# A written list of 1,373 steps in place of the list scheduler, and the first chunk loaded in three pieces

## The chip, the core and the metric

The kernel runs on one core of one Trainium2 chip. Its engines are TensorE (PE, which multiplies matrices into the eight PSUM banks), VectorE (DVE), ScalarE (ACT), GpSimd (POOL) and SyncE (SP, which here only issues transfers). Each engine works through its own list of instructions in order, and the engines wait for each other through semaphores. The metric is the device time of one execution in microseconds (us).

## The reference

```python
for t in range(S):                                   # gated linear attention
    state = alpha[:, :, t, :, None] * state + np.einsum('bhd,bhe->bhde', k[:, :, t], v[:, :, t])
    y[:, :, t] = np.einsum('bhd,bhde->bhe', q[:, :, t], state)
...
x = y.transpose(0, 2, 1, 3).reshape(B, S, H * D)     # then a mixture of 4 attention experts
logits = x @ w_gate                                  # the best 2 of 4, softmax over the two
for e in range(E):
    q = x @ wq[e]; k = x @ wk[e]; v = x @ wv[e]
    a = softmax(causal(scale * (q @ k.transpose(0, 2, 1))))
    out += weight[e] * (a @ v @ wo[e])
```

B is 4, H 8, S 768, D 48; the second part is 384 wide with 4 experts of 64.

## The kernel before

The sequence of every batch is cut into 6 chunks of 128 positions, 24 chunks in all, numbered n. Three chunks make a unit u of 384 positions, so there are 8 units and two to a batch. The work is about 1,370 small steps, each of one engine. In the text a step is called by the key that it has in the code:

- For chunk n, `La`, `Lq` and `Lv` load the gates, q with k, and v. DVE then prepares q and k: `r` and `c` are scans of the gates (L163, with a reciprocal L169 between them), `k` (L182) and `q` (L187) multiply by their results. `e` is a small copy on POOL. For n >= 3 `cp` moves a part of the tile T by two small transfers. Chunk 0 is prepared in pieces, so its steps carry a piece number.
- `a` (L204) forms the products of q and k on PE, the two `m` mask them (on DVE L208, or on ACT L212 and then POOL L216), `t` (L221) transposes k, `kt` (L225, L227) evicts it, `u` (L241) forms the chunk's addition to the state, `sa` (L254, DVE) and `S` (L258, POOL; L250 on DVE for the first) update the state, `y` (L280) is the chunk's output, `xh` (ACT) and `xl` (DVE L294) split it in a high and a low part. `ck` (ACT L196) is a check on the gates whose result is only needed at the end.
- `wqh`, `wql`, `wvh`, `wvl`, `woh`, `wol` split the weights in the same manner, once, near the start: the `h` on ACT (L672, L673, L678, L681), the `l` on DVE or POOL (L666, L674).
- For unit u, `p` (L303) is one of four q or k projections and `v` (L325) one of three v projections; `s` (L376) are scores, `rd`, `ex`, `n` and `ns` the softmax (DVE L388, ACT L399, DVE L405, POOL L411), `t` with four numbers (L426) transposes the probabilities, `to` evicts them into one of the buffers `at`, `o` (L451) multiplies them by v, `w` (L470) is the output projection, `wo` evicts and `st` stores it. `t4001` stands for unit 4, pair 0, tile 0, expert 1 of the pair.

What sets the order is the function `run`. It is a list scheduler that runs when the program is built: each step has a target time (made from the constants PACE and OFF), an estimated duration and the steps and buffers that it needs, and at each turn the step with the best mark is given to its engine, which sets the order of every queue, the engine of steps that have a choice, and the buffer of each tile. Where it reckons that PE would stand idle for longer than IDLE, it puts filler matmuls in (`warm`, L803, a 128x256 product whose result nobody reads). The loads of the start, 30 fillers and the order of the first transfers are written out in `opening`.

Of the kernel before, what the change touches and what calls it, by code (L numbers as in the profile page):

```python
# [33 lines left out]
PACE = 12.4037  # L34
PULL = {"P": 0.007, "V": 0.02, "A": 0.02, "G": 0.1134, "S": 0.1114}
SWITCH = 0.6006
CHANGE = {("t", "f"): 0.065, ("f", "t"): 0.0}
CHANGE.update({(x, "a"): 0.19 for x in "tfy"})
CHANGE.update({(x, "s"): 0.15 for x in "tfy"})
CHANGE.update({(x, "y"): 0.12 for x in "tfas"})  # L40
CHANGE.update({(x, "t"): 0.15 for x in "asy"})
CHANGE.update({(x, "f"): 0.2 for x in "asy"})
IDLE = 0.3647
SHARE = 0
HEAD = 0.0628
MARGIN = 0.3762
SLOW = 1.0555
OFF = dict(load=1.5592, prep=0.7084, a=-0.2534, y=0.0569, p=-0.066, pw=0.4525, v=-0.5128, g=0.5234, s=-0.069, step=0.9176, n=0.3117, tr=1.0059, o=0.2201, w=0.7913, wt=-1.9145, hp=1.0622, ck=0.6172, end=1.3946, hd=0.1337, sx=-0.1614, wo=0.0629, xo=-0.1397)
# [7 lines left out]
def tile_gla_moe(ctx: ExitStack, tc: tile.TileContext, qk_d, al_d, v_d, wqk_d, wv_d, wo_d, nat_d, vn_d, out_d):  # L56
# [32 lines left out]
    early = [[view(raw[0][:, 4 * CW * i:4 * CW * i + 4 * CW], 2, 2, CW) for i in (0, 1)]]  # L89
# [7 lines left out]
    def pieces(n):  # L97
        return [(0, 2), (2, 4)] if n == 0 else [(0, tiles(n))]
# [383 lines left out]
    def op(key, target, deps, alts, uses=(), take=(), mode="", land=0.0, lock=False):  # L482
        o = dict(key=key, target=target, deps=list(deps), alts=alts, uses=list(uses), take=list(take), mode=mode, land=land, lock=lock)
        ops.append(o)
        for n in o["uses"]:
            users[n] = users.get(n, 0) + 1
        return o
# [10 lines left out]
    def load_ops(n):  # L498
        z = (n - 3 - OFF["load"]) * PACE
        if n > HALF:  # L500
            op(("La", n, 0), z, [], [("S", 0.57, lambda: load_al(n, 0, SY))], [("al", n)], [("al", n)], land=3.7)
            op(("Lq", n, 0), z, [], [("S", 0.57, lambda: load_q(n, 0, SY))], [("T", n)], [("T", n)], land=4.2)
        if n >= HALF:
            op(("Lv", n), z, [], [("S", 0.57, lambda: load_v(n))], [("v", n)], [("v", n)], land=3.0)

    def scale(f, w, n, i):
        return [("V", dv(w), lambda: f(V, n, i))] + [("G", 0.12 + 0.0021 * w, lambda: f(G, n, i))] * (n < SHARE)

    def prep_ops(n):
        z = (n - 2 - OFF["prep"] + OFF["hp"] * max(0.0, 1.0 - (n - HALF) / 3) * (n >= HALF)) * PACE  # L510
        for i, (p0, p1) in enumerate(pieces(n)):
            k = p1 - p0
            past = [("c", n - 2, 0)] if n > 1 else []
            op(("r", n, i), z, [("La", n, i)] + past, [("V", 0.33 + 0.27 * k, lambda i=i: prep_r(n, i))], [("al", n)], lock=True)
            op(("e", n, i), z, [("r", n, i), ("Lq", n, i)], [("G", 0.19, lambda i=i: prep_e(n, i))], [("al", n), ("T", n)])
            op(("c", n, i), z, [("r", n, i)], [("V", 0.15 + 0.27 * k, lambda i=i: prep_c(n, i))], [("al", n)], lock=True)
            op(("k", n, i), z, [("r", n, i), ("Lq", n, i)], scale(prep_k, 128 * k, n, i), [("al", n), ("T", n)],
               lock=True)
            op(("q", n, i), z, [("c", n, i), ("Lq", n, i)], scale(prep_q, 128 * k, n, i), [("al", n), ("T", n)],
               lock=True)  # L520
        ready = [(x, n, i) for x in "ekq" for i in range(len(pieces(n)))]
        if n >= FIRST:
            op(("cp", n), z, ready, [("S", 1.15, lambda: spread(n))], [("T", n)], land=2.2)
            ready = [("cp", n)]
        op(("ck", n), z + OFF["ck"] * PACE, [(x, n, i) for x in "ekq" for i in range(len(pieces(n)))],
# [3 lines left out]
    def chunk_ops(n):  # L529
# [4 lines left out]
        head = OFF["hd"] if n < HALF else 0.0  # L534
        z = (n - 1 + OFF["a"] - head) * PACE
        op(("a", n), z, ready, [("P", 0.95, lambda: gla_a(n))], [("T", n)], [("pa", n, 0), ("pa", n, 1), ("ms", n)], "a")
        for s in (0, 1):
            op(("m", n, s), z, [("a", n)],
# [3 lines left out]
        if not last:  # L542
            op(("t", n), z, ready, [("P", 0.42, lambda: gla_t(n))], [("T", n)], [("pt", n)], "t")
            op(("kt", n), z, [("t", n)], either(gla_k, 448, n), [("pt", n)], [("kt", n)])
        z = (n + OFF["y"] - head) * PACE
        op(("y", n), z, [("m", n, 0), ("m", n, 1), ("Lv", n)] + ([("S", n)] if c else []),
           [("P", 1.55 if c else 0.95, lambda: gla_y(n))], [("T", n), ("v", n), ("ms", n)], [("py", n)], "y")
        zx = z + OFF["xo"] * PACE
        op(("xh", n), zx, [("y", n)], [("A", da(W3), lambda: gla_xh(n))], [("py", n), ("x", u)], [("x", u)] if g == 0 else [])
        op(("xl", n), zx, [("xh", n)], [("V", dv(W3), lambda: gla_xl(n))], [("py", n), ("x", u)])  # L550
        if not last:
            op(("u", n), z, [("kt", n), ("Lv", n)], [("P", 0.36, lambda: gla_u(n))], [("kt", n), ("v", n)], [("pu", n)], "y")
# [455 lines left out]
```

## Time and profile before

| | us |
|---|---|
| median of the runs shown (321.55 to 321.92) | 321.70 |
| the profiled execution | 322.28 |
| its span, first to last instruction | 320.5 |
| PE busy in the span | 307.3 |
| DVE busy | 266.7 |
| ACT busy | 195.3 |
| POOL busy | 125.2 |

The profiled execution is 0.58 us above the median of the runs, and 1.78 us of it lie outside the span. PE's ends are modelled, so a busy PE may still be one that waits a little.

### The profile page before, as it was taken

Reading aid. Unit: us, or ns where it says so; the run is one execution under the profiler, and the core shown is the slowest. Engines: PE = TensorE matmul, PEld = TensorE weight load, DVE = VectorE, ACT = ScalarE, POOL = GpSimd, SP = SyncE. Lnnn points to the kernel's source line nnn. Section 1 sums busy time; section 2 is a strip of 40 time slices with the busy share of each in tenths; the row PEclk is TensorE's granted clock in tenths of the full one; section 3 lists DMA queues with packets and bytes.
Section 4 is the critical chain, followed back from the end, with each engine's and each line's share of the span. In section 5 each row is a group of like instructions: output and inputs, shape, how many; then the busy total and the mean of one; then the engine's idle time right before and its main releaser. Section 6 shows DMA issues by size and latency. Waiting matters only on the chain.

```text
span 320.5 us, 11175 instructions
## 1 busy us (share of the span) xinstructions
PE 307.3 (96%) x4443; PEld 264.2 (82%) x4443; DVE 266.7 (83%) x767; ACT 195.3 (61%) x532; POOL 125.2 (39%) x205
## 2 busy tenths in 40 slices
PE   6798999999999999999999999999999999999992
PEld 4578988989897888889897887889897987878682
DVE  4997999999999999898998899898795785767840
ACT  1563657767674775557676685547584673457851
POOL 6351437514565372104363083405353070306420
PEclk9999999999999999999999999999999999999998
DMA  7994454724524514442534334322310000201001
GB/s 256 393 332 157 131 156 133 216 77 133 156 80 110 152 46 157 118 139 88 140 95 112 117 112 139 96 82 64 111 35 14 3 2 0 77 2 66 12 30 58
DMA packets 26638, 35.22 MB, mean 110 GB/s; under 512 B 2288, under 2 KB 22864, under 8 KB 26576
## 3 DMA queue, kind: packets, MB, share of 16 engines
q1 hardware_dynamic: 25744, 33.49, 34.1%
q10 hardware_dynamic: 832, 0.92, 0.9%
q8 instruction: 37, 0.61, 0.8%
q14 instruction: 25, 0.20, 0.2%
HBM read 27.61 MB, written 4.72 MB: 101 GB/s over the span
## 4 chain that ended last, share of the span: by engine, by line
PE 83%; DVE 11%; DMA 2%; issue 1%; ACT 1%; POOL 0%; ACTq 0%; SPq 0%; DVEq 0%; POOLq 0%
PE g L303 15%; PE g L426 12%; PE g L451 12%; PE g L376 9%; PE g L280 9%; PE g L325 8%; PE g L470 8%; PE g L204 5%; PE g L241 2%; PE g L221 2%; DMA at<-in_al_dram 2%; DVE a L388 2%; DVE a L163 2%; DVE T L187 1%; DVE T L182 1%
## 5 line engine op out<-in xcount | busy, mean ns | idle before, releaser
L411 POOL TENSOR_SCALAR a<-a,cf,gw 128x128 f32<-128x128 f32 (+5 forms) x96 | 72.6, 767 | 78.8 <-DVE cf L405 28.7
L399 ACT ACTIVATE a<-a,mx 128x256 f32<-128x256 f32 (+3 forms) x96 | 51.4, 536 | 6.9 <-DVE mx L388 6.7
L426 PE MATMUL g<-ident,a 128*128 128x128 f32 x336 | 52.7, 277 | 0.5 <-DVE at L227 0.4
L303 PE MATMUL g<-x,wqkh 128*128 128x384 f32 x192 | 51.9, 352 | 0.0
L426 PEld LDWEIGHTS g<-ident,a 128*128 128x128 f32 x336 | 39.2, 140 | 7.4 <-issue 4.9
L216 POOL TENSOR_SCALAR_AFFINE_SELECT ms<-ms 128x512 f32<-128x512 f32 x29 | 21.0, 733 | 56.0 <-ACT ms L212 56.0
L225 ACT ACTIVATE at<-g 128x512 f32<-128x512 f32 (+3 forms) x68 | 31.2, 473 | 17.1 <-PE g L426 15.7
L451 PE MATMUL g<-at,vg 128*32 128x384 f32 (+2 forms) x648 | 40.0, 389 | 0.0
L376 PE MATMUL g<-k,q 64*128 64x256 f32 (+3 forms) x384 | 39.2, 336 | 0.0
L227 DVE COPY at<-g 128x256 f32<-128x256 f32 (+3 forms) x60 | 27.6, 467 | 9.2 <-PE g L426 8.6
L451 PEld LDWEIGHTS g<-at,vg 128*32 128x32 f32 x648 | 19.3, 109 | 18.6 <-issue 14.8
L303 PEld LDWEIGHTS g<-x,wqkh 128*128 128x128 f32 x192 | 33.1, 189 | 1.2 <-DVE mx L388 0.4
L376 PEld LDWEIGHTS g<-k,q 64*128 64x128 f32 x384 | 28.6, 185 | 6.1 <-issue 2.2
L280 PE MATMUL g<-ms,v 128*32 128x128 f32 x768 | 33.0, 273 | 0.1
L303 PE MATMUL g<-x,wqkl 128*128 128x384 f32 x96 | 32.4, 338 | 0.0
L325 PE MATMUL g<-wvh,x 128*128 128x260 f32 x144 | 31.7, 295 | 0.3 <-DVE mx L388 0.3
L204 PE MATMUL g<-T 48*128 48x128 f32 x384 | 26.7, 277 | 4.2 <-DVE T L187 4.2
L204 PEld LDWEIGHTS g<-T 48*128 48x128 f32 x384 | 24.2, 187 | 6.2 <-DVE T L187 5.3
L388 DVE CUSTOM_DVE_ANT_0 a<-g,cmask 128x128 f32<-128x128 f32 (+3 forms) x64 | 28.2, 483 | 0.9 <-PE g L376 0.9
L470 PE MATMUL g<-woh,yy 128*128 128x384 f32 x96 | 27.9, 349 | 0.0
L258 POOL TENSOR_TENSOR S<-st,T 48x192 f32<-48x192 f32 x32 | 20.5, 639 | 16.0 <-DVE st L254 12.5
L212 ACT ACTIVATE ms<-g 128x512 f32<-128x512 f32 x29 | 16.4, 591 | 14.8 <-PE g L204 14.4
(113 smaller groups left out, 627.4 us busy)
## 6 DMA issues: line engine op xcount, KB each, us to landing
al<-in_al_dram SPq DMA_DIRECT2D x21, 387.0 KB, 3.8
T<-in_qk_dram SPq DMA_DIRECT2D x21, 384.0 KB, 4.1
v<-in_v_dram SPq DMA_DIRECT2D x24, 256.0 KB, 3.0
out_dram<-ot SPq DMA_DIRECT2D x22, 192.0 KB, 1.9
T<-T SPq DMA_DIRECT2D x42, 48.2 KB, 2.2
a<-in_al_dram SPq DMA_DIRECT2D x2, 516.0 KB, 6.8
T<-in_qk_dram SPq DMA_DIRECT2D x2, 512.0 KB, 7.5
at<-in_wqk_dram SPq DMA_DIRECT2D x1, 768.0 KB, 9.3
```

Of the source, the lines that this page charges most:

```text
L204: PE.matmul(pa[s][:, C * p:C * p + C], t[r:r + D, p, C:2 * C], t[r:r + D, p, 0:C], start=True, stop=True, tile_position=(r, 0))
L225: A.activation(out, src, AF.Copy)
L280: PE.matmul(o[32 * j:32 * j + 32, k], l, r, start=(i == 0), stop=(i == len(parts) - 1), tile_position=(0, 32 * j))
L303: PE.matmul(pj[:, :W3], w[:, kt, cs], x[:, kt, :], start=(i == 0), stop=(i == 8))
L325: PE.matmul(pv[:, 0:260], x[:, kt, 128 * i:128 * i + 128], w[:, kt, :], start=(m == 0), stop=(m == 8))
L376: PE.matmul(sc(u, pair, i, e, x, c1 - c0), q[r, i0, ts], k[r, i1, c0:c1], start=(y == 0), stop=(y == 2), tile_position=(64 * e, 0))
L388: V.tensor_tensor_reduce(a[:, c0:c1], src, cmask[:, 512 - c1 + c0:512], -1.0, mx[:, 0:1] if x else 3.0e38, OP.add, OP.min, mx[:, 1:2])
L399: A.activation(a[:, c0:c1], src, AF.Exp, bias=mx[:, 1:2], scale=-1.0 if last else 1.0, accum_out=sm[:, x:x + 1])
L411: G.tensor_scalar(a[:, 0:n], a[:, 0:n], CF[u % 2][:, 3 * pair + i, e:e + 1], gw[:, u, i, eg:eg + 1], op0=OP.mult, op1=OP.mult)
L426: PE.transpose(pt[:, 128 * (j - j0):128 * (j - j0) + 128], a[:, 128 * j:128 * j + 128], ident)
L451: PE.matmul(o[r:r + 32, lo:n1], v[:, j % 3, 64 * eg + x:64 * eg + x + 32], at(("at", u, pair, e))[:, min(j, 4), at_off(j) + lo:at_off(j) + ...
L470: PE.matmul(po[:, 0:DM], y[:, h, 128 * i:128 * i + 128], w[:, pair, :], start=(m == 0), stop=(m == 5))
```

## The change

The scheduler, its constants and all estimates of time are gone from the order. In their place stands the text QUEUES, a list of 1,406 words: the 1,373 steps, of which 28 come in two halves, and fillers at 5 places. Each word is an engine's letter and the number of a step (P PE, V DVE, A ACT, G POOL, S SP; `z11` is 11 fillers). The new `run` gives out the steps in just that order. A buffer is taken from the front of a list of free ones and goes to the back of it when its last user has been issued. Beside that:

- Chunk 0 is loaded and prepared in three pieces of one, two and one of its four tiles (OPEN) and not in two of two.
- The first transfers of SP come in another order (ORDER): the weights wv ahead of wqk.
- The check `ck` of the first three chunks has to come after `wqh` (LATE).
- The tile pools `at` and `q` have 3 and 2 buffers, and had 4 and 3.

```diff
-PACE = 12.4037
...
+OPEN = [(0, 1), (1, 3), (3, 4)]
+LATE = 'wqh'
+ORDER = [(0, 1), (1, 0), (0, 2), (1, 1), (2, 1), (2, 0), (1, 2), (0, 3), (2, 2)]
+UNITS = dict(a=7, at=3, ms=2, kt=2, x=2, q=2, k=4, yy=2, vg=3, T=4, al=3, v=3, ot=2, st=2)
+
+QUEUES = """
+S1 S4 V68 V70 V71 G69 V72 V73 V75 V78 G74 V76 V77 G79 V80 V81 V82 V94 P84 P87 G95 A85 V86 A88 V96 z1 P92 V97 G85 V98
...
-        return [(0, 2), (2, 4)] if n == 0 else [(0, tiles(n))]
+        return OPEN if n == 0 else [(0, tiles(n))]
...
-    def run(start, arrive):
...
+    def run():
         left = dict(users)
+        spare = {k: list(range(len(unit[k]))) for k in unit}
...
+        for word in QUEUES.split():
+            e, i = word[0], int(word[1:])
+            if e == "z":
+                warm(spare["g"][0], i)
+                continue
+            o = ops[i]
...
             for name in o["take"]:
                 pool = POOL.get(name[0], name[0])
+                where[name] = (pool, spare[pool].pop(0))
             alt[2]()
             for name in o["uses"]:
+                left[name] -= 1
+                if left[name] == 0:
+                    pool, i = where[name]
+                    spare[pool] += i if isinstance(i, tuple) else (i,)
```

On DVE, from the first instruction on, the preparation of chunk 0 stood so before (`at_63` holds the gates of chunk 0, `T_85` its q and k; the scans are called SCALAR_TENSOR_TENSOR here):

```order
L163 SCALAR_TENSOR_TENSOR at_63<-at_63,d1r 128x258
L169 RECIPROCAL d1c_109<-at_63 128x2
L163 SCALAR_TENSOR_TENSOR at_63<-at_63,d1c_109 128x258
L182 TENSOR_TENSOR T_85<-T_85,at_63 128x2x128
L163 SCALAR_TENSOR_TENSOR at_63<-at_63,d1r 128x258
L169 RECIPROCAL d1c_109<-at_63 128x2
L187 TENSOR_TENSOR T_85<-T_85,at_63 128x2x128
```

and stands so now (L215 are the scans, L234 and L239 the products):

```order
L215 SCALAR_TENSOR_TENSOR at_63<-at_63,d1r 128x129
L221 RECIPROCAL d1c_107<-at_63 128x1
L215 SCALAR_TENSOR_TENSOR at_63<-at_63,d1c_107 128x129
L234 TENSOR_TENSOR T_83<-T_83,at_63 128x128
L239 TENSOR_TENSOR T_83<-T_83,at_63 128x128
L215 SCALAR_TENSOR_TENSOR at_63<-at_63,d1r 128x258
L221 RECIPROCAL d1c_107<-at_63 128x2
```

The first piece is half as wide, and chunk 0 takes 15 instructions of DVE where it took 10.

On POOL, after the first small copies, the weights' low parts stood so before (`ms` are the masked products, `S` and `st` the state):

```order
L173 COPY T_86<-a 128x4
L216 AFFINE_SELECT ms_67<-ms_67 128x512 x2
L216 AFFINE_SELECT ms_68<-ms_68 128x512
L173 COPY T_87<-a 128x4
L216 AFFINE_SELECT ms_68<-ms_68 128x512
L258 TENSOR_TENSOR S_113<-st_97,T_87 48x4x48 x2
L666 TENSOR_TENSOR wvl<-at_65,wvh 128x780
L173 COPY T_88<-al_89 128x3
```

and stand so now (L225 is the copy, L268 the mask, L310 the state, L701 the weights):

```order
L225 COPY T_84<-a 128x4
L268 AFFINE_SELECT ms_66<-ms_66 128x512
L225 COPY T_85<-a 128x4
L268 AFFINE_SELECT ms_67<-ms_67 128x512 x2
L701 TENSOR_TENSOR wvl<-at_65,wvh 128x780
L310 TENSOR_TENSOR S_111<-st_95,T_85 48x4x48 x2
L701 TENSOR_TENSOR wqkl<-at_64,wqkh 128x3x256
L701 TENSOR_TENSOR wol<-at_65,woh 128x768
L225 COPY T_86<-al_87 128x3
```

One of the four masks has gone to DVE, wvl comes ahead of the state, and the splits wqkl and wol, which were DVE's, stand on POOL ahead of the copy for chunk 3.

On PE, in the middle of the program, unit 4's first transposes stood so before (`a` are probabilities, `T2` and `T3` the tiles of chunks 18 and 19, the first name the PSUM bank):

```order
L426 MATMUL g7_107<-ident_111,a_99 128x128 x2
L221 MATMUL g4_104<-ident_111,T2_87 128x112 x4
L426 MATMUL g0_100<-ident_111,a_99 128x128
L221 MATMUL g6_106<-ident_111,T3_88 128x112 x4
L426 MATMUL g7_107<-ident_111,a_99 128x128
L280 MATMUL g5_105<-ms1_68,v2_94 32x128 x4
```

and stand so now (L478 the transposes of probabilities, L273 that of k, L355 a projection):

```order
L478 MATMUL g6_104<-ident_109,a_97 128x128
L478 MATMUL g1_99<-ident_109,a_97 128x128
L273 MATMUL g0_98<-ident_109,T2_85 128x112 x4
L478 MATMUL g3_101<-ident_109,a_97 128x128 x2
L478 MATMUL g2_100<-ident_109,a_97 128x128 x2
L355 MATMUL g4_102<-x1_71,wqkh_128 128x384 x2
```

Before, the second transpose of unit 4's first pair (the last L426 row, t4001) writes the bank g7 of the transposes that ended unit 3 (the first row, t3121), with two `t` and t4000 between them. Now t4000 and t4001 stand together, the next tile's two follow after one `t`, and each of the six rows has a bank of its own.

## Rows read from the trace of the kernel before

**Rows 1.** The page: busy time and the chain by engine.

```profile
PE 307.3 (96%) x4443; PEld 264.2 (82%) x4443; DVE 266.7 (83%) x767; ACT 195.3 (61%) x532; POOL 125.2 (39%) x205
...
PE 83%; DVE 11%; DMA 2%; issue 1%; ACT 1%; POOL 0%; ACTq 0%; SPq 0%; DVEq 0%; POOLq 0%
```

**Rows 2.** Stretches of the span: length, then busy time (instructions) by engine.

```profile
0.00:27.10 27.10, 20.34 (x367) 16.45 (x368) 20.85 (x35) 12.61 (x22) 13.27 (x33) 1.00 0.89 313
27.10:51.00 23.90, 23.47 (x349) 21.27 (x348) 23.22 (x64) 14.03 (x39) 7.88 (x15) 1.00 0.54 157
51.00:304.00 253.00, 252.53 (x3567) 216.90 (x3563) 218.93 (x659) 162.28 (x457) 101.70 (x156) 1.00 0.30 88
304.00:315.00 11.00, 10.94 (x176) 9.54 (x168) 3.69 (x11) 5.93 (x15) 2.39 (x3) 1.00 0.08 25
```

**Rows 3.** All waits of PE: total, times, longest.

```profile
PE g L204 <- DVE T L187: 4.2, 4, 1.6
PE g L803 <- POOL ones L137: 1.5, 1, 1.5
PE g L241 <- issue: 1.0, 1, 1.0
PE g L426 <- DVE at L227: 0.4, 1, 0.4
PE g L325 <- DVE mx L388: 0.3, 1, 0.3
```

**Rows 4.** PE in order of time: start, duration, [idle before, releaser].

```profile
1.55 5.01 PE L803 MATMUL g<-d1r 128*128 128x256 bf16 x30 [1.55 <-POOL ones L137]
8.20 0.72 PE L204 MATMUL g<-T 48*128 48x128 f32 x8 [1.64 <-DVE T L187]
...
14.09 1.16 PE L204 MATMUL g<-T 48*128 48x128 f32 x16 [1.46 <-DVE T L187]
...
19.34 1.16 PE L204 MATMUL g<-T 48*128 48x128 f32 x16 [0.55 <-DVE T L187]
...
25.57 0.28 PE L241 MATMUL g<-v,kt 128*32 128x48 f32 x7 [1.03 <-issue]
25.78 1.59 PE L803 MATMUL g<-d1r 128*128 128x256 bf16 x13
27.13 0.37 PE L325 MATMUL g<-wvh,x 128*128 128x260 f32 x1
...
28.29 0.52 PE L303 MATMUL g<-x,wqkh 128*128 128x384 f32 x2
...
33.66 0.72 PE L803 MATMUL g<-d1r 128*128 128x256 bf16 x5
34.30 1.16 PE L204 MATMUL g<-T 48*128 48x128 f32 x16
```

**Rows 5.** DVE in order of time.

```profile
4.85 0.78 DVE L163 TENSOR_TENSOR_SCAN at<-at,d1r 128x258 f32<-128x258 f32 x1 [2.83 <-DMA at<-in_al_dram]
...
9.32 1.22 DVE L163 TENSOR_TENSOR_SCAN a<-a,d1r 128x516 f32<-128x516 f32 x1
...
11.94 1.06 DVE L182 TENSOR_TENSOR T<-T,a 128x512 f32<-128x512 f32 x1
...
16.19 1.47 DVE L163 TENSOR_TENSOR_SCAN a<-a,d1c 128x516 f32<-128x516 f32 x1
17.59 0.66 DVE L182 TENSOR_TENSOR T<-T,a 128x512 f32<-128x512 f32 x1
...
20.60 1.29 DVE L208 TENSOR_TENSOR ms<-g,mask 128x512 f32<-128x512 f32 x2
...
22.67 0.95 DVE L666 TENSOR_TENSOR wqkl<-at,wqkh 128x768 fp32r<-128x768 f32 x1
23.57 0.56 DVE L294 TENSOR_TENSOR x<-g,x 128x384 fp32r<-128x384 f32 x1
25.97 0.74 DVE L254 TENSOR_TENSOR st<-g,S 48x192 f32<-48x192 f32 x2 [1.84 <-PE g L241]
```

**Rows 6.** POOL in order of time.

```profile
11.19 2.30 POOL L216 TENSOR_SCALAR_AFFINE_SELECT ms<-ms 128x512 f32<-128x512 f32 x2 [0.40 <-ACT ms L212]
15.95 0.63 POOL L216 TENSOR_SCALAR_AFFINE_SELECT ms<-ms 128x512 f32<-128x512 f32 x1 [2.46 <-ACT ms L212]
...
20.28 1.09 POOL L258 TENSOR_TENSOR S<-st,T 48x192 f32<-48x192 f32 x2 [1.54 <-DVE st L254]
23.30 2.04 POOL L666 TENSOR_TENSOR wvl<-at,wvh 128x780 fp32r<-128x780 f32 x1 [1.92 <-issue]
```

**Rows 7.** PE in the middle: two of its longer waits, and t7100.

```profile
47.73 0.39 PE L325 MATMUL g<-wvh,x 128*128 128x260 f32 x1 [0.34 <-DVE mx L388]
...
190.87 0.30 PE L426 MATMUL g<-ident,a 128*128 128x128 f32 x1 [0.39 <-DVE at L227]
...
304.07 1.64 PE L426 MATMUL g<-ident,a 128*128 128x128 f32 x13
```

More of the change, by code (lines that the diff above doesn't have):

```diff
@@ L33 @@
 FIRST = 3
-PACE = 12.4037
[L35 to L48, printed above, removed]
@@ L480, in tile_gla_moe, with op @@
     ops, users = [], {}
-    def op(key, target, deps, alts, uses=(), take=(), mode="", land=0.0, lock=False):
-        o = dict(key=key, target=target, deps=list(deps), alts=alts, uses=list(uses), take=list(take), mode=mode, land=land, lock=lock)
+    def op(key, deps, alts, uses=(), take=(), mode="", land=0.0, lock=False):
+        o = dict(key=key, deps=list(deps), alts=alts, uses=list(uses), take=list(take), mode=mode, land=land, lock=lock)
         ops.append(o)
@@ L522, in prep_ops @@
         if n >= FIRST:
-            op(("cp", n), z, ready, [("S", 1.15, lambda: spread(n))], [("T", n)], land=2.2)
+            op(("cp", n), ready, [("S", 1.15, lambda: spread(n))], [("T", n)], land=2.2)
             ready = [("cp", n)]
-        op(("ck", n), z + OFF["ck"] * PACE, [(x, n, i) for x in "ekq" for i in range(len(pieces(n)))],
+        op(("ck", n), [(x, n, i) for x in "ekq" for i in range(len(pieces(n)))] + [(LATE,)] * (n < HALF),
            [("A", 0.28 + 0.0021 * 129 * tiles(n) * 0.8, lambda: check(n))], [("al", n)])
@@ L598, in back_ops @@
             first = hf or i == 0
-            z = (base + step * k) * PACE
             if hf:
@@ L615, in back_ops @@
                 time = sum(3 * max(c1 - c0, 256) / 2170 for ii in tiles3 for c0, c1 in widths(u, ii)) + 0.05
-                op(scored, z, need + past, [("P", time, lambda p=pair, l=tiles3: [score(u, p, ii) for ii in l])],
+                op(scored, need + past, [("P", time, lambda p=pair, l=tiles3: [score(u, p, ii) for ii in l])],
                    [("q", u, pair), ("k", b, pair)], take, "s")
@@ new lines, in run @@
+                spare[pool].remove(j)
+        begun = set()
+        for word in QUEUES.split():
[4 more added lines that the diff above has]
+            o = ops[i]
+            if i in begun:
+                next(alt[3] for alt in o["alts"] if len(alt) > 3)[2]()
+                continue
+            alt = next(alt for alt in o["alts"] if alt[0] == e)
+            if len(alt) > 3:
+                begun.add(i)
@@ L781, in run @@
-            if e == "G":
-                lock["G"].append((t, end))
-            if e == "P":
-                mode = o["mode"] or mode
-            end += o["land"]
-            for name in o["uses"]:
-                give(name, end, e)
-            if len(alt) > 3:
-                k = dict(key=o["key"], target=o["target"], deps=[("half", o["key"])], alts=[alt[3]], uses=[], take=[], mode="", land=0.0,
-                         lock=False, n=0)
-                done["half", o["key"]] = (end, e)
-                cand.append(k)
-                continue
@@ L794, in run @@
-            done[o["key"]] = (end, e)
-            todo -= 1
-            for w in waiting.get(o["key"], ()):
-                w["n"] -= 1
-                if not w["n"]:
-                    cand.append(w)
+            for name in o["uses"]:
+                left[name] -= 1
+                if left[name] == 0:
+                    pool, i = where[name]
+                    spare[pool] += i if isinstance(i, tuple) else (i,)
     def warm(i, k):
```

303 lines of the change are left out of this document (126 added, 177 removed).

## The prediction

> **What bounds the kernel now.** The page says that PE is busy for 307.3 of 320.5 us, and the chain that ended last runs 83% on PE and 11% on DVE [rows 1]. PE's work as such is the same after the change: the same products of the same shapes. So time can come only from where PE has nothing useful to do, and I read where that is. The table by stretches shows PE busy for 20.34 of the first 27.1 us, for 23.47 of the next 23.9, for 252.53 of 253 in the middle and for 10.94 of 11 at the end [rows 2]. The list of PE's waits says the same: 4.2 us before the products `a` of the first chunks, 1.5 before the first filler, 1.0 in an `u`, and 0.7 in all the rest [rows 3]. The first stretch also holds 68 of the fillers, so the opening is the place to look at first.
>
> The same table shows why the opening is slow. Through 27.1 to 51 us DVE is busy for 23.22 of 23.9 us [rows 2], and in PE's rows each of the first chunks' `a` (8.20, 14.09, 19.34) waits for DVE's product `q` [rows 4]. DVE starts when the first gates land, at 4.85, and has one pause in the opening, 1.84 us ahead of the row at 25.97 [rows 5]. Until some 50 us it is DVE's work that lets PE go on.
>
> A modelled end of a matmul hides short waits, so I also went through PE's rows start to start. Between v00 (27.13, [rows 4]) and the start of t7100 at 304.07 [rows 7] stand 292 steps. I compared each with the shortest time that the same step takes after the same kind of step. What they lie above that adds up to 4.1 us: 1.0 by 51 us, and 3.1 after it in some 25 pieces, of which the longest is 0.55 around the row at 190.87; the row at 47.73 shows the longest of the first kind [rows 7]. That is all that a better order can win in the middle.
>
> **The change, part by part.**
>
> Chunk 0 in three pieces. DVE takes 15 instructions for 10. A scan of 258 columns takes 0.78 and one of 516 takes 1.22 [rows 5], so a third piece costs what does not shrink with width, about 0.2 us for the first scan and 0.1 to 0.2 for each of the other four, 0.6 in all. Against it stands an earlier start: the first transfer is half as large. I take 0.25 us for that; the bounds are 0 and 0.45 (half of its 264 KB at the rate of the stretch, 313 GB/s [rows 2], is 0.42). So DVE is through with chunk 0 some 0.35 us later than now (9.32).
>
> From there I walked DVE's new queue with the durations of its old rows: `r` of chunk 1 to 11.0, the mask that has come from POOL (half of 1.29) to 11.7, `c` to 12.9, `k` and `q` to 14.2 (0.66 each) or 15.0 (1.06 each, as beside POOL's mask now [rows 5, 6]), chunk 2's scans with xl0 and the first state to about 19.5, `q` of chunk 2 to 20.1, sa1, wql and an eviction of 0.5 to 21.9, two masks to 23.1, xl1 to 23.6. The scans of chunk 3 follow at once; they start at 27.2 now. DVE has this room because wqkl and wol (0.95 each) have gone to POOL and because its pause of 1.84 us is filled.
>
> PE on this walk: y1 when the first state is there, at 19.5, to 21.0; t2 and a2 to 22.5; u2; then v00 at 22.9, and not at 27.13. Now v00 stands behind 13 fillers, which take from 25.78 to 27.13 although wvl, its last input, is ready at 25.34 [rows 4, 6]. That wait of 1.35 us goes for certain. `wvh` and wvl come earlier too: ACT does wvh right behind chunk 1's masks, since the checks `ck` have been put behind wqh, and wvl stands ahead of the state on POOL. PE then does y2 (needs the masks at 23.1 and the state S2, 1.09 behind sa1 [rows 6], at 21.7) and is through with it at about 25.5. Now it has done the same steps at 28.29, where p000 starts [rows 4]. The lead is 2.8 us. PE goes on with v01, p001, v02, p011, p000 and gets to a3 at about 33; chunk 3's spread lands at about 31.5, so nothing waits there. The fillers there are 4 for 5, worth 0.1. **The opening gives 2.8 us.** Below, the certain part is the 1.35 less 0.35 and some 0.3 lost elsewhere, 0.7; above, with the unhindered products and a start at 4.4, it is 4.0.
>
> POOL's added work: wvl takes 2.04 us, so wqkl and wol take about 2.0 each with their 768 columns [rows 6]. They stand between the state S2 (done at 21.7) and the copy `e` of chunk 3, so they end at 25.7. The copy has to be done before chunk 3's spread, which waits for DVE's `k` at about 28. That hides them with 2 us to spare. If that cover is gone, a3 is late by the excess, and the projections ahead of it hide another 1.5.
>
> The middle. Two things speak for less waiting. First, rows that wait now have another place: t4001 waits for DVE's eviction from the bank that t3121 has just left, 0.39 us [rows 7], and now writes a bank that none of the rows shown uses. Second, I counted PE's work between the score step and the transposes that need it, from the two orders with each step's present duration. Its median over 96 pairs is 9.5 us now and 13.7 us after, its smallest 4.1 and 5.5. More work stands between a step and the one that waits for its softmax. Against it: the buffers `at` are 3 for 4, so the pair's second transpose must follow the last pair's `o` on PE, and the order no longer adapts to anything. The shortest cover between a last transpose and its `o` is 0.8 us for an eviction of some 0.6, against 0.5 now. The bounds are a gain of 4.1 (no wait is left) and a loss of 1 (as much again as the middle now loses by 51 us). **I take 1.5**, nearer to the middle of the two, since 3.1 of the 4.1 lie in waits of about 0.1 us that any order has in part.
>
> Work by kind of step: PE pays about 0.1 us when it changes between whole-array, row-split and column-split products. From v00 on I count 99 such changes now and 97 after. Nothing.
>
> SP: the same transfers in another order; in the rows its loads run some chunks ahead, so I cost it at nothing. If a load of v or q comes late, PE waits for its landing, about 3 us. The end: t7120 and what follows have the same steps in nearly the same order, and PE's stretch from 304 to 315 has 0.06 us idle [rows 2]. Nothing.
>
> **Sum.** 2.8 + 1.5 = 4.3 us. Span 320.5 - 4.3 = 316.2; the profiled execution 322.28 - 4.3 = 318.0; it lies 0.58 above the median of the runs, so 317.4.
>
> **The rivals.**
>
> *POOL and DVE get in each other's way.* Two rows speak for it: beside POOL's masks DVE's product `k` takes 1.06 for 0.66 and a scan 1.47 for 1.23, and two of POOL's masks take 2.30 where one alone takes 0.63 [rows 5, 6]. If DVE's scan of chunk 3, ready at 23.6, is held until POOL's two splits are done at 25.7, xl2 and the projections come 2.1 us later: 319.5. Against it: the rows show delays of a quarter to a half, and xl1 ran at its usual 0.56 inside wvl (23.57, [rows 5, 6]). [...]
>
> *The lead is lost again by 51 us, and the middle stays as it is.* DVE is full until then [rows 2], and what it gains by moved work it gives back through 5 more instructions, an eviction and a mask. Then only the 0.7 is left: 321.0. For it speaks that PE's idle time after 27 us is 0.9 us by the table. Against it speaks DVE's pause of 1.84.
>
> *All waits go.* Opening 4.0 and middle 4.1: 313.6.
>
> [...]
>
> **How the numbers follow.** Forecast 0.58, POOL against DVE 0.12, lead lost 0.13, all waits gone 0.08, clock or another thing that makes it slower 0.09. The prediction is 317.4. The range goes from 314.4 (most of what can be won) to 321.1, which takes in the lost lead; it leaves out the slower case and part of the best. About 0.2% (0.64 us) is what a measurement can tell from no change, so the bound to faster is 321.06. The lost lead lies on it, half to each side: faster 0.84, same 0.07, slower 0.09.
>
> **What would show it.** In the opening: 49 fillers in all, v00 between 22.5 and 24.5, y2 done before 26.5, a3 at about 33, and DVE without its pause of 1.84. If v00 is early and a3 is not, the lead was lost on DVE or POOL: then POOL's L666 instructions last longer than 2.04 or DVE's scans of chunk 3 start after 25.5. In the middle: PE's busy share in the 253 us stays, its steps move up by 4 us at the end against 3 at 60 us, and the wait at t4001 is gone. If the lead at 60 us is larger than at the end, the fixed order made new waits; I would look at `o` waiting for evictions, then at late loads. [...]

## The result and the profile after

The changed kernel takes 325.55 us (median of 6 runs, 324.86 to 326.21), the kernel before on the same chip 321.82 (321.55 to 322.03). The ratio is 1.0116, with a 95% interval of 1.01 to 1.0132: 3.7 us slower, where I had forecast 4.3 faster. The profiled execution takes 325.54 with a span of 323.7; both are 3.2 to 3.3 above those of before.

The chain that ended last, of the changed kernel, shares of the span by engine; PE's share was 83% [rows 1]:

```profile
PE 65%; DVE 23%; issue 4%; DMA 3%; ACT 2%; SPq 0%; POOL 0%; DVEq 0%; POOLq 0%; ACTq 0%
```

Busy time by stretches of the changed kernel (columns as in [rows 2]: the stretch, its length, then busy time and instructions of PE, PE's weight loads, DVE, ACT and POOL, granted clock, DMA share, GB/s):

```profile
0.00:27.10 27.10, 22.40 (x361) 17.42 (x362) 22.64 (x41) 11.91 (x21) 15.68 (x35) 0.94 0.90 313
27.10:51.00 23.90, 22.72 (x399) 20.76 (x401) 23.23 (x66) 11.66 (x32) 8.38 (x18) 1.00 0.43 118
51.00:304.00 253.00, 250.51 (x3467) 216.07 (x3459) 210.44 (x632) 161.62 (x474) 96.81 (x152) 1.00 0.30 91
304.00:315.00 11.00, 10.98 (x198) 8.49 (x190) 6.69 (x20) 4.84 (x14) 3.69 (x4) 1.00 0.08 28
315.00:318.50 3.50, 2.50 (x20) 2.06 (x12) 0.34 (x2) 1.26 (x3) 0.00 (x0) 1.00 0.19 57
```

In the middle PE stands idle for 2.49 us of 253, where it was 0.47 [rows 2]. At 315 us, where the kernel before was done with PE, 2.50 us of PE's work are still to come. PE's list of waits says on whom (engine and line, released by whom and where, total, times, longest):

```profile
PE g L256 <- DVE T L239: 2.0, 1, 2.0
PE g L760 <- POOL ones L189: 1.6, 1, 1.6
PE g L478 <- DVE mx L440: 0.9, 2, 0.5
PE g L355 <- DVE x L346: 0.6, 1, 0.6
...
PE g L428 <- DVE mx L440: 0.3, 1, 0.3
PE g L355 <- DVE mx L440: 0.3, 1, 0.3
PE g L478 <- POOL a L463: 0.3, 1, 0.3
PE g L377 <- DVE mx L440: 0.3, 1, 0.3
PE g L522 <- DVE mx L440: 0.2, 1, 0.2
```

The first rows are the opening's. What is new is `mx L440`: DVE's read of the scores (`rd`), for which transposes, projections, the output product and later score steps wait. None of them needs its result; they are to write the PSUM bank that it still reads. Two places in PE's rows:

```profile
168.22 0.49 PE L478 MATMUL g<-ident,a 128*128 128x128 f32 x3
169.07 0.63 PE L478 MATMUL g<-ident,a 128*128 128x128 f32 x4 [0.37 <-DVE mx L440]
169.98 0.62 PE L355 MATMUL g<-x,wqkh 128*128 128x384 f32 x2 [0.28 <-DVE mx L440]
...
186.75 0.33 PE L355 MATMUL g<-x,wqkl 128*128 128x384 f32 x1
187.41 0.80 PE L428 MATMUL g<-k,q 64*128 64x128 f32 x3 [0.33 <-DVE mx L440]
```

and what DVE did ahead of the second:

```profile
184.08 0.48 DVE L440 CUSTOM_DVE_ANT_0 a<-g,cmask,mx 128x256 f32<-128x256 f32 x1
184.49 0.08 DVE L440 DVE_READ_ACCUMULATOR2_ANT mx<- 128x1 f32 x1
184.49 1.44 DVE L215 TENSOR_TENSOR_SCAN al<-al,d1r 128x387 f32<-128x387 f32 x1
185.96 0.18 DVE L221 RECIPROCAL d1c<-al 128x3 f32<-128x3 f32 x1
186.05 0.66 DVE L438 TENSOR_REDUCE mx<-g 128x1 f32<-128x512 f32 x1
186.86 0.48 DVE L440 CUSTOM_DVE_ANT_0 a<-g,cmask,mx 128x256 f32<-128x256 f32 x1
187.27 0.08 DVE L440 DVE_READ_ACCUMULATOR2_ANT mx<- 128x1 f32 x1
```

A scan for a later chunk stands between two reads of scores, and here it takes 1.44 us for the usual 0.95, beside two of POOL's masks:

```profile
184.47 1.88 POOL L268 TENSOR_SCALAR_AFFINE_SELECT ms<-ms 128x512 f32<-128x512 f32 x2 [4.59 <-ACT ms L264]
```

PE's next score step starts as the last of these reads ends.

How far ahead is a kernel at a given time? I added up PE's steps in the order of each trace, each at the shortest time it takes in the trace of before, and looked when the kernel before had done as much. Positive is ahead of before, in us:

| at (us) | 28 | 60 | 100 | 140 | 180 | 220 | 280 | 310 |
|---|---|---|---|---|---|---|---|---|
| changed kernel | 1.8 | 2.3 | 1.0 | 0.5 | -1.3 | -1.8 | -1.9 | -2.8 |
| e1, new start, old order behind | 2.0 | 2.5 | -3.9 | -3.9 | -3.9 | -3.6 | -3.6 | -4.6 |
| e2, old order, new rule for banks | 0.3 | 0.3 | 0.3 | 0.3 | 0.3 | 0.8 | 0.8 | 0.3 |
| e7, 17 moves on DVE | 1.0 | 1.7 | 0.9 | 0.5 | -0.4 | 0.0 | 0.0 | -0.6 |
| e8, two pieces | 2.1 | 2.7 | 1.4 | 0.9 | -0.2 | -0.2 | -0.3 | -0.9 |
| e16, others anew behind 60 | 1.7 | 2.3 | 1.6 | 1.1 | 0.2 | 0.7 | 0.8 | 0.4 |
| e15, all anew behind 60 | 1.5 | 2.6 | 1.1 | 0.8 | 0.1 | 0.6 | 1.0 | 1.2 |

The opening gave its 2.3 us; between 60 and 310 us 5.1 were lost.

### The profile page after: what moved, and what is told of

It is laid out like the page before. It is cut to its first block, busy times and chain, and to the rows that moved or that the text cites. A ratio compares the mean times of both kernels' runs of the same rounds, so it can differ in the third digit from the quotient of the medians.

```text
span 323.7 us, 11041 instructions
## 1 busy us (share of the span) xinstructions
PE 309.1 (95%) x4419; PEld 264.8 (82%) x4419; DVE 263.3 (81%) x758; ACT 191.3 (59%) x544; POOL 124.6 (38%) x207
## 4 chain that ended last, share of the span: by engine, by line
PE 65%; DVE 23%; issue 4%; DMA 3%; ACT 2%; SPq 0%; POOL 0%; DVEq 0%; POOLq 0%; ACTq 0%
PE g L503 11%; PE g L355 11%; PE g L478 9%; PE g L428 8%; PE g L332 8%; PE g L377 6%; PE g L522 6%; DVE al L215 5%; PE g L256 4%; DVE a L440 2%; DMA T<-in_qk_dram 2%; DVE mx L438 2%; DVE st L306 2%; DMA at<-in_al_dram 1%; PE g L293 1%
## 5 line engine op out<-in xcount | busy, mean ns | idle before, releaser
L463 POOL TENSOR_SCALAR a<-a,cf,gw 128x128 f32<-128x128 f32 (+5 forms) x96 | 72.3, 763 | 111.9 <-DVE cf L457 71.2
L451 ACT ACTIVATE a<-a,mx 128x256 f32<-128x256 f32 (+3 forms) x96 | 51.6, 539 | 15.2 <-DVE mx L440 15.1
L355 PE MATMUL g<-x,wqkh 128*128 128x384 f32 x192 | 51.1, 346 | 0.9 <-DVE x L346 0.6
L478 PE MATMUL g<-ident,a 128*128 128x128 f32 x336 | 44.4, 275 | 1.2 <-DVE mx L440 0.9
L277 ACT ACTIVATE at<-g 128x128 f32<-128x128 f32 (+3 forms) x82 | 32.6, 438 | 15.8 <-PE g L478 15.5
L478 PEld LDWEIGHTS g<-ident,a 128*128 128x128 f32 x336 | 37.5, 140 | 4.4 <-POOL a L463 2.4
L355 PEld LDWEIGHTS g<-x,wqkh 128*128 128x128 f32 x192 | 33.7, 188 | 2.5 <-DVE x L346 0.9
L332 PE MATMUL g<-ms,v 128*32 128x128 f32 x768 | 34.6, 280 | 0.4 <-POOL ms L268 0.3
L355 PE MATMUL g<-x,wqkl 128*128 128x384 f32 x96 | 32.5, 338 | 0.0
L451 ACT ACTIVATE a<-g,mx 128x384 f32<-128x384 f32 (+1 forms) x32 | 20.2, 632 | 17.3 <-DVE mx L440 17.3
L268 POOL TENSOR_SCALAR_AFFINE_SELECT ms<-ms 128x512 f32<-128x512 f32 x28 | 19.4, 700 | 26.6 <-ACT ms L264 26.3
L440 DVE CUSTOM_DVE_ANT_0 a<-g,cmask 128x384 f32<-128x384 f32 (+3 forms) x64 | 28.2, 484 | 1.7 <-PE g L428 0.9
L522 PE MATMUL g<-woh,yy 128*128 128x384 f32 x96 | 28.9, 350 | 0.2 <-DVE mx L440 0.2
L279 DVE COPY at<-g 128x512 f32<-128x512 f32 (+3 forms) x46 | 22.9, 528 | 5.7 <-PE g L478 5.3
L310 POOL TENSOR_TENSOR S<-st,T 48x192 f32<-48x192 f32 x32 | 17.9, 558 | 22.2 <-DVE st L306 21.0
```

The source lines that it names most:

```text
L277: A.activation(out, src, AF.Copy)
L332: PE.matmul(o[32 * j:32 * j + 32, k], l, r, start=(i == 0), stop=(i == len(parts) - 1), tile_position=(0, 32 * j))
L355: PE.matmul(pj[:, :W3], w[:, kt, cs], x[:, kt, :], start=(i == 0), stop=(i == 8))
L440: V.tensor_tensor_reduce(a[:, c0:c1], src, cmask[:, 512 - c1 + c0:512], -1.0, mx[:, 0:1] if x else 3.0e38, OP.add, OP.min, mx[:, 1:2])
L451: A.activation(a[:, c0:c1], src, AF.Exp, bias=mx[:, 1:2], scale=-1.0 if last else 1.0, accum_out=sm[:, x:x + 1])
L463: G.tensor_scalar(a[:, 0:n], a[:, 0:n], CF[u % 2][:, 3 * pair + i, e:e + 1], gw[:, u, i, eg:eg + 1], op0=OP.mult, op1=OP.mult)
```

## The experiments

The runs stand on several chips, so each is given by its ratio to the kernel before on the same chip; the changed kernel's is 1.0116.

**e1. The new start with the old order behind it.** The first 240 words stay; all other steps follow in the order of the kernel before.

```diff
-UNITS = dict(a=7, at=3, ms=2, kt=2, x=2, q=2, k=4, yy=2, vg=3, T=4, al=3, v=3, ot=2, st=2)
+UNITS = dict(a=7, at=4, ms=2, kt=2, x=2, q=3, k=4, yy=2, vg=3, T=4, al=3, v=3, ot=2, st=2)
-QUEUES (words 241 on)
+QUEUES (the remaining steps in the order of the kernel before)
```

> The first 240 words of the new list (to about 60 us), then all remaining steps in the order of the kernel before; 4 buffers at and 3 q as before. Theory A (the loss is in the new list's order after 60 us): the lead of 2.35 us at 60 us stays, 321.8 - 2.3 = 319.5. Theory B (the loss comes from the rule that takes banks from the front of a free list, whatever the order): the lead goes again as in the changed kernel, 321 to 324.

326.93 us, 1.0147 (1.0125 to 1.0169): neither. The seam itself cost 6.4 us between 60 and 100 us; the old order had other steps done by then, PE stood idle for 3.15 of the 41.00 us of the first stretch, and the granted clock had a mean of 0.96 there. By stretches:

```profile
51.00:92.00 41.00, 37.85 (x513) 32.80 (x506) 33.83 (x99) 27.00 (x77) 15.49 (x27) 0.96 0.49 142
92.00:304.00 212.00, 211.54 (x2925) 181.93 (x2924) 180.49 (x550) 133.14 (x375) 82.83 (x126) 1.00 0.28 82
```

Behind the seam PE is busy for 211.54 of 212 us and loses nothing against before from 100 to 280 us (table), where the changed list loses 2.9. As a whole the run missed; this part speaks for theory A.

**e2. The old order with the new rule for banks.** QUEUES, OPEN and ORDER hold what the scheduler had given out, and UNITS is the line of e1.

```diff
-OPEN = [(0, 1), (1, 3), (3, 4)]
+OPEN = [(0, 2), (2, 4)]
```

> The scheduler's own order, engines and fillers, word for word as in the kernel before, chunk 0 in two pieces, 4 at and 3 q; only the choice of the bank and buffer is the new rule's (front of the free list). Theory A (order): as before, 321.8 within 0.3. Theory B (bank rule): waits for banks held by score reads as in the changed kernel, 1 to 3 us slower, 323 to 325.

322.11 us, 1.0007 (0.9992 to 1.0022). Theory B falls: taking banks from the front of a list costs nothing in the old order.

**e3. Other banks in the new order.**

```diff
-                where[name] = (pool, spare[pool].pop(0))
+                where[name] = (pool, spare[pool].pop(spare[pool].index(next(banks)) if pool == "g" else 0))
```

> The changed kernel's list as it is; only the bank of each step is written out: of the banks free in the list's order the one that came free earliest in the trace of the changed kernel. Theory B (bank rule): the waits at 76.7, 84.7 and 187.4 us, where an earlier bank was free, go, up to 2.0 us, 323.5 to 324.3. Theory A (order): most waits are for banks of which no other was free earlier, 325.0 to 325.6. Theory C (fewer buffers): no change, 325.5.

324.85 us, 1.0069 (1.0046 to 1.0092), its runs from 322.82 to 327.41: between the two. A better choice of banks helps the new order somewhat. In the profiled execution, the slowest of these runs, the waits at 84.7 and 187.4 us are gone; the transposes of 76.7 us now wait for their own input `ns`, and the projection of 169.98 waits for the same read of scores as in the changed kernel.

**e4. More buffers.** The line of UNITS as in e1, and nothing else.

> The changed kernel with 4 buffers at and 3 q, as before the change, and nothing else. Theory C (the transposes wait for one of only three buffers at, or a product for one of two q): 2 us or more come back, 323.5 or less. Theories A and B: no change, 325.3 to 325.8, since the rows of the waits name banks.

325.60 us, 1.0095 (1.0064 to 1.0125). Theory C falls.

**e5. Fillers for the clock.**

```diff
-        warm(7, 30)
+        warm(7, 44)
```

> The changed kernel with 44 fillers at the start for 30, which fill most of the 2.0 us in which PE waits between the two parts of a0, and 4 for 1 ahead of u0. Theory D (PE's clock, which falls at 12.4 us after that pause, costs time): the granted clock stays 1.00 from 10 to 18 us, y0 takes 1.08 for 1.94, and 0.7 to 1.5 us come back, 324.0 to 324.8. Rival: DVE is the bound there and hides it, 325.3 to 325.8.

325.66 us, 1.0103 (1.0083 to 1.0122): no gain. The stretches from 12 to 16 and from 24 to 28 us, first of the changed kernel:

```profile
12.00:16.00 4.00, 4.00 (x67) 2.96 (x55) 3.97 (x7) 1.04 (x2) 0.19 (x1) 0.57 1.04 405
24.00:28.00 4.00, 3.96 (x75) 3.32 (x73) 3.93 (x5) 1.07 (x4) 4.00 (x3) 1.00 0.51 143
```

and of e5:

```profile
12.00:16.00 4.00, 3.75 (x89) 2.94 (x90) 3.97 (x7) 1.77 (x4) 0.26 (x2) 1.00 1.04 403
24.00:28.00 4.00, 4.00 (x57) 3.68 (x61) 3.93 (x5) 0.00 (x0) 4.00 (x3) 0.57 0.33 107
```

The clock held at 12 us and fell at 24 instead.

**e6. wol later on POOL.**

```diff
-... V130 G67 A123 ...  G136 P156 ...
+... V130 A123 ...  G136 G67 P156 ...
```

> The changed kernel with wol on POOL behind the mask of chunk 3 (at 39 us, where POOL stands idle for 3 us) and not at 24.75 us beside DVE's scans of chunk 3. Theory E (POOL holds DVE up there): the second scan takes about 1.2 for 2.19 us, PE's wait of 0.87 ahead of p001 goes, 324.6 to 324.9. Rival: what is won is lost at the next wait for DVE, at 42.5 us, 325.3 to 325.8.

327.11 us, 1.0162 (1.0128 to 1.0195), slower than theory and rival had it. The scan is as short as foreseen, and another scan is long at the new place; that this is the whole loss is not shown. DVE's rows of e6:

```profile
25.76 0.96 DVE L198 TENSOR_TENSOR_SCAN al<-al,d1c 128x387 f32<-128x387 f32 x1
...
37.75 2.52 DVE L198 TENSOR_TENSOR_SCAN al<-al,d1c 128x387 f32<-128x387 f32 x1
```

and POOL's:

```profile
37.61 1.84 POOL L684 TENSOR_TENSOR wol<-at,woh 128x768 fp32r<-128x768 f32 x1
```

**e7. DVE's order alone.** 17 of DVE's words, given here with their places in the list:

```
rd4020 896>880  rd1010 320>323  r21 835>837  c13 492>507  q10 357>340  sa10 468>472
sa13 688>680  sa22 1143>1138  g1 4 812>796  g3 5 1007>1012  g3 6 1192>1163  n112 476>477
n312 850>846  m71 317>324  kt13 657>658  pl410 869>847  to30211 773>768
```

> The changed kernel with 17 of DVE's steps moved by up to 30 words behind 42 us (three steps of chunk preparation, the first at 84 us, later or earlier; score reads, evictions and parts of the softmax to the other side of them); the order of PE, ACT, POOL and SP is the same word for word, and so are the opening and the buffers. Theory A (the loss behind 60 us is the order, above all DVE's, which gives banks and inputs back too late): the waits at 76.7, 84.7, 164 to 170, 187 and 296 to 309 us shrink, 2.5 to 3.1 us, 322.4 to 323.0. Theory B or C (bank rule, buffers): 325.2 to 325.8.

323.64 us, 1.0048 (1.0030 to 1.0066). Of 5.1 us lost behind 60 us, 2.8 are back (table: 1.7 to -0.6, a loss of 2.3). In the profiled execution the opening was 0.6 worse, and the time missed the range foreseen. Theory A holds in kind: no step of PE was moved.

**e8. Chunk 0 in two pieces.** OPEN as in e2, the words of the third piece left out.

> The changed kernel with chunk 0 in two pieces as before; everything else in its place. If the three pieces cost what their 5 more DVE instructions take less the earlier start (my 0.35 us): DVE is through with chunk 0 that much earlier than at 9.94, 325.0 to 325.3. If the earlier start is worth more, it is slower, 325.7 to 326.2. If the pause in PE that three pieces make drops the clock, it stays at 1.00 from 10 to 18 us, and it is 1 us faster, 324.5.

324.71 us, 1.0075 (1.0056 to 1.0093): by its ratio better than any of the three ways foreseen, and the sign of the third did not come: the granted clock fell all the same, from 11.7 to 15.1 us (0.50 from 12 to 15). 0.4 us of the gain are there at 60 us, near my estimate of 0.35; most of the rest comes at 160 to 190 us, where the waits ahead of the rows at 169.07, 169.98 and 187.41 are gone. Nothing but small shifts ahead of them tells the two lists apart there: a step with so little room waits or not by a few tenths of a us.

**e9. The splits off POOL.**

```diff
-... G65 V115 ... V62 ... G63 A116 ... V128 S6 V130 G67 ...
+... V115 ... V62 V65 ... V128 V63 S6 V130 ... (G67 behind the copy e of chunk 7)
```

65 is wvl, 63 wqkl, 67 wol.

> The changed kernel with the three splits taken off POOL's way: wvl and wqkl on DVE (behind wql, and behind the first scan of chunk 3; 0.95 us each), wol on POOL behind the copy e of chunk 7, at 54 us. Theory E (POOL's splits and DVE's scans and products shut each other out, 18 to 28 us): c of chunk 3 takes 0.95 for 2.19, r 0.95 for 1.48, PE's wait of 0.87 ahead of p001 goes, 0.9 us by 35 us, and the runs lie closer together; 324.3 to 325.0. Rival (DVE has no room for 1.9 us more): v00 waits for wvl, 326 or more.

324.93 us, 1.0079 (1.0061 to 1.0098), runs from 324.19 to 325.53. The time lies where theory E had it, its reason does not show: the second scan took 0.96, but DVE's own work put `v00` at 24.18 us for 23.13, at 35 us PE was 0.1 behind the changed kernel, and the runs lie as far apart as those (1.34 and 1.35 us). Where the gain comes from stays open.

**e10, e11, e12, e13, e14. Lists ordered anew from 20 us on.** In e10 and e11 the second half of a mask comes behind its `y` in 17 chunks, so that there `y` reads products that are not masked yet; e12 to e14 do all the work. All five have chunk 0 in two pieces and the buffers of e1.

```diff
-QUEUES = """ (the changed kernel's 1,406 words)
+QUEUES = """ (the same steps from t of chunk 2 on in another order)
```

> The list with chunk 0 in two pieces, and from t of chunk 2 (20.5 us) on ordered anew: single steps moved or put on another engine, against the durations that the traces of before and after show, with 0.12 us from engine to engine, and POOL's and DVE's SBUF work one after the other; judged at these durations and at 3% longer ones, so that PE's inputs and banks come with some room. 4 at and 3 q; no fillers behind y1. Theory A (what the changed kernel loses behind 60 us is its order, and an order can avoid it): the lead of 2.6 us at 60 us stays, 321.1; with the 3.1 us of waits of the kernel before gone too, 318. Rival (a written order loses to run-to-run differences whatever it is): 324 or more.

> The searched list with 44 fillers at the start for 30, and 4 for 1 ahead of u0. Theory D (the clock's drop behind 12 us costs up to 1.5 us where it isn't hidden): the clock stays 1.00 from 10 to 18 us, 0.3 to 1.5 us faster than the searched list without them. Rival (DVE and POOL set the pace there, or the drop only moves to the next pause, as it did to 24 us with the changed list): within 0.3 us of it.

> The changed kernel with chunk 0 in two pieces and PE's order kept word for word; from t of chunk 2 (20.5 us) on the steps of DVE, ACT, POOL and SP are ordered anew (and evictions with a choice put on the other engine) against the durations of the traces, with 0.12 us from engine to engine, POOL's and DVE's SBUF work one after the other, each mask done ahead of its product y, and some room: judged at the durations read and at 3% longer ones. 4 at, 3 q, no fillers behind y1. Theory A (the waits that the changed list makes behind PE's back can be taken out by the other engines' order): about half of some 8.5 us of waits go, 324.7 - 4.4 = 320.3. Rival (PE's own order makes them): 323 or more.

> As the kernel with the other engines' order, but PE's steps are moved too. Theory A: more room and fewer changes of PE's kind of product, 2 us or more below the kernel with PE's order kept, 317.5 to 318.5. Rival (what one gains by moving PE's steps is lost to waits that the durations don't show): the same or slower than it.

> The kernel with the other engines' order, with 44 fillers at the start for 30, 4 for 1 ahead of u0 and 5 more ahead of u2. Theory D (the clock's drop in the opening costs time): the granted clock stays 1.00 until 30 us and it is 0.3 to 1.5 us faster than without them. Rival: DVE and POOL set the pace up to 30 us, within 0.3 us.

325.27, 326.47, 326.82, 325.40 and 329.11 us; 1.0106, 1.0146, 1.0122 (1.0105 to 1.0139), 1.0090 (1.0075 to 1.0104), 1.0192. None came where theory A or D had it. e12 and e13 lost some 2 to 3 us between 38 and 51 us, ahead of products `u`, `y` and `a`. In e12 PE stood for 2.19 us ahead of the `u` at 40.64, and then the granted clock was 0.51 from 41.4 to 44.9 us; in e13 the longest wait, 0.97 us, was for the transfer `cp`. The durations that I ordered by did not tell of these waits, and why they came stays open. The number that the rival gave for e10 and e12 came out, but e15 and e16 below speak against its reason. Behind 60 us e13 lost only 1.3. e14 held the clock at 1.00 up to 30 us, as asked, and was still the slowest.

**e15, e16. Ordered anew behind 60 us alone.**

```diff
-QUEUES = """ (from word 264 on, SP's words apart)
+QUEUES = """ (e16: DVE, ACT and POOL in another order; e15: PE too)
```

Both start from the list of e8 with the buffers of e1, and leave out its last two fillers. e8 alone is at 1.0075, and the buffers alone (e4) won nothing.

> The changed kernel with chunk 0 in two pieces, word for word until 60 us; behind that the steps of PE, DVE, ACT and POOL are ordered anew against the durations of the traces (0.12 us from engine to engine, POOL's and DVE's SBUF work one after the other, masks ahead of their product, room for loads and for 3% longer steps); SP's order is kept; 4 at and 3 q. Theory A (the loss behind 60 us is the order): the lead of 2.7 us at 60 us stays to the end, where the run with two pieces alone was 0.9 behind: 324.7 - 3.6 = 321.1, and to 319.5 with PE's steps packed closer. Rival (a written order loses in the middle whatever it is): 323 or more.

> As the one before, but PE's order is the changed kernel's word for word throughout; only DVE, ACT and POOL are ordered anew behind 60 us. Theory A, with the order of the engines that PE waits for as the cause: at least the 1.9 to 2.9 us that 17 moves on DVE gave, 324.7 - 2.9 = 321.8, 321.0 to 322.8. Rival (PE's order): 323.5 or more.

e15: 320.66 us, 0.9965 (0.9945 to 0.9984), faster than both kernels. e16: 322.42 us, 1.0025 (1.0011 to 1.0039). Both came where theory A had them. The middle of e15, then of e16:

```profile
51.00:304.00 253.00, 251.88 (x3504) 216.53 (x3493) 213.09 (x638) 166.02 (x482) 105.27 (x154) 1.00 0.31 91
```

```profile
51.00:304.00 253.00, 252.43 (x3507) 217.21 (x3496) 213.16 (x638) 166.49 (x484) 103.71 (x154) 1.00 0.30 92
```

In e16, with PE's order word for word the changed kernel's, its idle time there is 0.57 us for 2.49. In e15, 1.00 of the 1.12 idle us is one wait for a transfer. `mx` is gone from e15's list of waits; in e16's one of 0.2 us is left.

**e17. The kernel before without the 13 fillers ahead of `v00`.** e2 with one word less.

```diff
-... z13 P490 ...
+... P490 ...
```

> The kernel before, in its own order by the written list, without the 13 fillers ahead of v00, which I took for a wait of 1.35 us that goes for certain. If it carries on: v00 at 25.8 for 27.1, 320.8. If DVE, full from 27 to 51 us, sets when a of chunk 3 and what follows can go (the rival of the lost lead): 321.8 to 322.4, v00 early and the row at 47.7 where it was.

322.56 us, 1.0020 (1.0005 to 1.0035): nothing won. PE's rows: `v00`, `a3` and the row that [rows 7] has at 47.73:

```profile
25.27 0.39 PE L360 MATMUL g<-wvh,x 128*128 128x260 f32 x1
...
32.78 1.26 PE L239 MATMUL g<-T 48*128 48x128 f32 x16
...
47.20 0.39 PE L360 MATMUL g<-wvh,x 128*128 128x260 f32 x1 [0.48 <-DVE mx L423]
```

1.86 us early, then 1.52, then 0.53: the lead melts while DVE is full.

## Why the prediction was wrong

**The step that failed is the middle: "I take 1.5" of a gain, bounds 4.1 and a loss of 1.** It was a loss of 5.1. Three things were wrong in it.

The bound below. I took the waits of the kernel before as all there was to win or lose. A new order makes waits that no row of before shows; the bound held only if it made none.

The measure. I counted PE's work between a score step and the transposes that need its softmax, and that cover did grow: `ns L463` stands in PE's list of waits with 0.3 us. What the list no longer gave room is the other direction, a bank's last reader and the step that writes the bank next. For each PE step between 62 and 304 us I took the time from the end of its last input, or of the last reader of its bank, on another engine to its start. It is under 0.3 us in 19 of 254 steps before and in 45 of 254 after. `rd` is the last in 4 of them before and in 13 after, an input in 1 before and in 11 after. The count goes with the loss: e2 18, e15 22, e16 32, e7 36, e8 41. So does the time. Start to start, against the shortest time of the same kind of step in the trace of before, these close steps stand 2.1 us too high before and 7.4 after: 5.9 behind a bank's reader, 3.6 of it behind `rd` (before 0.3), and 1.5 behind an input. All other steps stand 16.9 us too high before and 16.4 after, so the loss of this stretch lies at the close steps. The counts place the loss; that the order does it is shown by e7, e15 and e16, and that the rule for banks alone does not by e2.

The direction of the choice. t4001's wait is gone, as foreseen. I took one known wait gone as a sign for the whole. And no new order that ran won any of the 4.1 in the middle: the best, e15, lost 1.4 behind 60 us.

**The end**, costed at nothing, lost about 0.9 of the 5.1 behind 280 us, the most of it at 295.8 (0.4, an input `ns`) and 300.5 us (0.4, a bank that `rd` reads); e15 and e16 lose 0 to 0.4 there. Another 0.6 us lies behind PE's last product: ACT's issue of the last store lasts 1.49 us, before 0.78. Why stays open.

**The opening**, 2.8, came to 2.3 at 60 us: the size was nearly right. `v00` is at 23.13 us (22.9), `y2` is through at 26.16 (25.5), DVE's pause is gone, there are 49 fillers. `a3` is not early: it starts at 34.82 us, foreseen at 33 and before at 34.30. My own sign would call the lead lost by that; it is not, since PE has done one projection more by then (`p011`, at 31.16 us and before at 41.36). The third piece cost DVE 0.40 us (chunk 0 is through at 9.94, in e8 at 9.54) for my 0.35, by luck in part: the two rows of 0.78 and 1.22 us give 0.34 for what does not shrink in a scan, and I took 0.2. And the "certain part" was wrong in kind: e17 shows that the 1.35 us ahead of `v00` are worth nothing alone. What keeps the lead behind `v00` is then other work that was moved; I take it to be DVE's, but no run takes that apart, and in e9, where two of the splits are DVE's again, little of it goes (0.1 us at 35 us).

**The rivals.** POOL against DVE is real, at less than its 2.1 us; DVE's and POOL's rows around chunk 3:

```profile
24.14 1.48 DVE L215 TENSOR_TENSOR_SCAN al<-al,d1r 128x387 f32<-128x387 f32 x1
25.66 0.18 DVE L221 RECIPROCAL d1c<-al 128x3 f32<-128x3 f32 x1
25.87 2.19 DVE L215 TENSOR_TENSOR_SCAN al<-al,d1c 128x387 f32<-128x387 f32 x1
```

```profile
22.94 1.86 POOL L701 TENSOR_TENSOR wqkl<-at,wqkh 128x768 fp32r<-128x768 f32 x1
24.75 2.49 POOL L701 TENSOR_TENSOR wol<-at,woh 128x768 fp32r<-128x768 f32 x1
```

The scans take 1.48 and 2.19 for 0.95, and PE's L355 waits 0.6 us for `xl2` behind them. Of the 0.09 for the clock or another thing, the clock's part came true too, and cost little: 0.57 granted from 12 to 16 us, `y0` in 1.94 us for 1.08. I take it that DVE's pace hid most of that: e11, which holds the clock that fell in e10, won nothing, nor did e14 (in e5 it only fell later); no run shows the price of the lower clock alone. Of the changed kernel's own runs, one with a mean granted clock of 1.000 took 324.86 us, one with 0.998 took 326.21. Neither explains the 5.1 behind 60 us: the granted clock is 1.00 there, and from 62 to 304 us DVE's scans and products lie 2.2 us in sum above their usual times after, 2.1 before and 4.0 in e15.

The forecast's own marker did: it said that a lead larger at 60 us than at the end means new waits of the fixed order. It sent me to `o` and to late loads, and it was the banks.

## What to carry to other kernels

A change of order is not bounded by the waits that the old order shows: count how many steps would start within a few tenths of a us of their last release, for inputs and for buffers that come free, and expect trouble from a count that doubles (here 19 and 45). A written order should have room at each such place, above all for late reads of a shared buffer behind long work on a busy engine, and two halves of different orders can't simply be joined where their queues differ (e1, 6.4 us). A wait at one step is worth its length only if the engine that sets the pace behind it is moved too.

## What the runs showed of the hardware

DVE's scans and POOL's work held each other up. In e6 `wol` ends at 37.61 + 1.84 = 39.45, and the scan begun at 37.75 ends at 40.27, 0.82 later, though alone it takes 0.96. In the changed kernel `wol` ends at 24.75 + 2.49 = 27.24 and the scan at 25.87 + 2.19 = 28.06, again 0.82 later; the scan before it ends at 25.62, 0.82 after `wqkl` at 24.80. In the traces of before and of the changed kernel 17 scans of 128x387 began with 0.16 us or more of a POOL instruction still to run. 16 of them ended 0.81 to 0.83 us after that instruction and took 0.97 to 2.19; one (before, 202.16) took 0.94, and the POOL multiply begun 0.14 us ahead of it took 1.29, where the mean of its line's 96 is 0.77. The scans with no POOL instruction beside them took 0.94 to 0.96.

Who goes first differs between executions: `q` of chunk 2 started ahead of `wvl` in the changed kernel's profile and took 0.95 us, `wvl` 2.29; in e3, e5 and e7, with the same words up to there on DVE and POOL, `wvl` started first and took 1.86, `q` 2.19. The runs of e3 lie 4.6 us apart, those of the kernel before 2.0.

PE's clock was granted at 0.50 in the changed kernel from 12.18 to 15.59 us (0.57 as a mean from 12 to 16 us), behind a pause of 2.0 us at 7.3 us. With that pause filled (e5) it fell at 24 us, behind one of 1.39 us; in e7, which has both pauses (2.09 and 1.39), it stayed at 1.00. In e8 it fell at 11.7 us with no pause over 1.47 us behind the first filler, and the kernel before, with 1.64 and 1.46, kept it. So in these runs the length of a pause alone does not tell whether the clock falls. In the changed kernel it rose again at 15.6 us, while PE was busy for all of the 4.00 us from 12 to 16.

Two figures that the forecast and the expectations use, as the trace of before shows them. Between 28 and 304 us, where PE stood idle for less than 0.15 us in between, the first product of the next step started 0.20 us (median of 12) after the last product of a `y` when the kind of product changed and 0.09 (of 9) when it did not, and after that of a `p` 0.26 (of 4) and 0.17 (of 28): about 0.1 for the change. In 281 waits of one engine for another, the waiting instruction started 0.06 us (median) after the end of the one that released it, in eight of ten 0.03 to 0.18; the 0.12 was my allowance.
